# Attention opening: q of batch 0 in 24-token runs, a whole first FFN chunk, and a new order of the instructions

## The chip, the cores and the metric

The kernel runs on one core of a Trainium2 chip. A core has five engines that run their own instruction lists and wait for one another by semaphores: TensorE (PE, with its weight loads shown apart as PEld), VectorE (DVE), ScalarE (ACT), GpSimd (POOL) and SyncE (SP). The metric is the device time of one execution in microseconds, as the median of the runs shown.

## The reference

Two parts are computed, one behind the other. The attention works on 4 batches, 8 heads, 768 tokens and 64 dimensions, with the tokens in 8 blocks of 96. A small matrix per head says how key and value blocks are mixed:

```python
P = sort_net
for _ in range(5):
    P = P - np.max(P, axis=-1, keepdims=True)
    P = np.exp(P)
    P = P / (np.sum(P, axis=-1, keepdims=True) + 1e-09)
    P = P / (np.sum(P, axis=-2, keepdims=True) + 1e-09)
k_sorted = np.einsum('bhij,bhjcd->bhicd', P, k_b)
v_sorted = np.einsum('bhij,bhjcd->bhicd', P, v_b)
scores = scale * np.matmul(q_b, k_sb.transpose(0, 1, 2, 4, 3))
attn = softmax(scores)            # within the block of 96 only
x = attn @ v_sb                   # to (3072 tokens, 512)
```

The feed-forward part takes these 3,072 rows of 512:

```python
h = x @ w_in                      # 512 -> 2048
g = np.maximum(h, 0.0) + alpha * np.minimum(h, 0.0)
out = g @ w_out                   # 2048 -> 512
```

## The kernel before

All work goes by 32 groups, one for each batch and block (group 8 is the first of batch 1). For a group PE makes two kinds of scores. In the near form, used for batch 0, the scores are made twice: once as rows for the maximum (L715 in two halves of the array, DVE takes the maximum at L721) and once turned, with the negative maximum added by a product (L736, L727), so that one exp on ACT (L759) gives the turned matrix that the product with V needs (L768). In the far form, used from batch 1 on, PE makes them once (L712), ACT makes eight exps (L748), and SP turns the result by DMA (L753). DVE divides by the row sums (L776, L779), and xq is turned on PE (L794) or by DMA (L787) into xT.

Ahead of it stand the mixing matrices. The Sinkhorn loop (L518 to L532) alternates between ACT (the exp, L521) and DVE. Its result Pb is spread by eight products (L539) into BDK, with which batch 0's K is mixed and turned in one step: six units of 16 products (L600, written to PSUM) and one copy each (L372, into KT). V of batch 0 goes the same way in eight units (L653 copies, L674 products, L372 copies into VS). For later batches the mixing takes units of 8 products (K: L616, L629, L640; V: L658, L669, L684); a "piece" below is one such unit.

q of batch 0 is loaded by POOL (L397) and turned on PE in six units of 16 products against the identity (also L600), with an ACT copy each (L372, into QTz). q of later batches is loaded by POOL in eight pieces, one for each head (L401, into QN), and turned by six DMA transposes on SP (L409), each of which needs all eight pieces.

The feed-forward part works on chunks of groups. FFN1 (L823) is one unit of four products for each of the 16 slices of the 2,048 columns, on 192 tokens (two groups) or 384 (four groups). ACT takes relu(−h) (L833) and DVE makes the result (L836). FFN2 (L863) sums 16 products of 512 columns for each 128 tokens, in four groups of four, and the result is copied out (L372) and stored by SP (L877).

Loads are issued by POOL (q L397; K and V L419 and L435; w_in in four parts L908; w_out in two parts L913) and go through one queue in order.

The order is written out by hand. SEQ is a list of the numbers of all operations; each engine runs its operations in the order of that list, and a letter behind a number picks the engine where two can do it. The costs and priorities that each operation carries in the code have no part in it. WARM puts filling products ahead of operations of PE: 512-wide products of the identity (L808) into a bank that nobody reads. BURST is a run of small products of zeros (L889) at the very start. PSUM banks are named psS, psH, psO, psYP and so on.

Of the kernel before, what the change touches and what calls it, by code (L numbers as in the profile page):

```python
# [7 lines left out]
AP = bass.AP  # L8
# [19 lines left out]
BURST = 130  # L28
# [8 lines left out]
0 7 11 2 3 1 4 8 9 22 42 28 14 43 44 45 46 19 47 18 5 48 49 50 15 51 39 52 53 6 54 55 25 56 138 57 58 23 29 59 12p  # L37
60 61 130 62 63 64 31 65 32 66 37 13 67 68 89 69 83 81 70 84 71 87 131 10 91 88 85 132 72 40 73 90 74 133 75 86 76
41 77 82 134 78 79 92 26 80 147 93 148 102 94d 103a 104 95 105a 100 98 96a 99a 97d 109d 106p 35 111d 112d 108p 34
16 101a 36 38 33 107p 158 149 114 115d 146 110p 118 250p 159 116 248p 119a 120 113p 121d 124 30 117d 160 135 125a  # L40
249p 254p 24 136 161 122 137 144 150 126 127a 143 123d 145 128 151 129d 253p 247d 20 17 152 162 21 163 164 141 153
177 154 140 155 165 156 142 166d 184 157a 167 185 196 193 168 186 169 194 197 195 199 198 187 202 170 27 203 205
200 204 188 201 214 206 220 215 217 189 218 207 221 219 222 226 216 229 190 227 223 230 273 228 224 171 208 231 225
235 191 236 238 192a 237 232 239 261 251 262 209 313p 233 252a 240 210 263 347p 211 139 255 241 270 234 212 403 264
256a 213d 291 404 301d 271 242 175 259 292 258p 274 260a 257p 272 265 352p 267 243 266 279 244 311p 293 280 268
300p 281 282 269 312p 294 245 174 304d 285 310p 246d 275 286 351p 283 287 284 338 348p 302 339 295 305p 303a 314
288 296 315 306 289 316 340 307a 290 176 297 320 341 317 276 318 178 321 319 298 322 379 299a 308 380 323 179 309a
342 326 324 343 349 344 327 381 350a 325 328 345 353 382 346d 329 354d 332 330 383 333 331 357 277a 334 180 335
# [982 lines left out]
```

## Time and profile before

| | |
|---|---|
| median of 3 runs | 238.37 us (237.72 to 238.66) |
| span of the profiled execution | 236.6 us (the page gives no other time for it) |
| PE busy | 229.2 us, 97% of the span |
| DVE, ACT, POOL busy | 169.8, 151.6, 73.0 us |
| first score product (L715) | 17.72 us |
| first FFN1 product (L823) | 28.71 us |
| first FFN2 product (L863) | 36.40 us |
| first score product of group 8 (L712) | 56.88 us |

Times in the profile are microseconds from the start of the span. A timeline row has the start, the duration, the engine, the line, what is written from what, the shape and the count; in brackets stands how long the engine was idle before it and what released it, where that was long enough to be shown. "issue" as a releaser means that the profile shows nothing that the engine waited for. Matmuls overlap, so a row's duration is longer than its step to the next row.

### The profile page before, as it was taken

What the parts mean: (1) busy time and instruction counts of PE and PEld (TensorE: products, weight loads), DVE (VectorE), ACT (ScalarE), POOL (GpSimd) and SP (SyncE); (2) the same over time, 40 slices, a digit from 0 to 9 for tenths busy, and PEclk for the clock granted to TensorE, in tenths of its full rate; (3) what the DMA queues carried; (4) which work ended last, traced back from release to release, by engine and by line L of the source; (5) the groups of instructions that cost most, each with busy time, mean ns of one, the idle gap of its engine ahead of it and who ended that gap; (6) DMA issues with size and microseconds to landing.
All of it is one profiled execution on the core that took longest, in us unless ns stands there. A gap on an engine that the chain in (4) does not pass through costs nothing.

```text
span 236.6 us, 6266 instructions
## 1 busy us (share of the span) xinstructions
PE 229.2 (97%) x2532; PEld 142.2 (60%) x2532; DVE 169.8 (72%) x354; ACT 151.6 (64%) x423; POOL 73.0 (31%) x139
## 2 busy tenths in 40 slices
PE   7998998999999999999999999999999999999995
PEld 3446676687666666556566665655555555555543
DVE  4748796989899997868887667676766587744350
ACT  4475265587887988886678786756864646453332
POOL 7958812915659620338590020000000000000000
PEclk9999999999999999999999999999999999999999
DMA  5999999999989999899998796542642323400033
GB/s 96 212 213 168 211 217 202 179 209 158 191 88 167 152 120 173 119 210 166 165 111 114 188 164 135 98 90 52 125 92 82 97 50 79 140 0 1 0 133 135
DMA packets 71453, 31.36 MB, mean 133 GB/s; under 512 B 64504, under 2 KB 65280, under 8 KB 71424
## 3 DMA queue, kind: packets, MB, share of 16 engines
q0 software_dynamic: 22896, 13.63, 42.0%
q1 hardware_dynamic: 48528, 17.33, 37.8%
q8 instruction: 20, 0.33, 0.5%
q14 instruction: 9, 0.07, 0.1%
HBM read 27.28 MB, written 6.29 MB: 142 GB/s over the span
## 4 chain that ended last, share of the span: by engine, by line
PE 76%; DMA 17%; POOL 6%; issue 1%; ACT 0%; POOLq 0%
PE psH L823 31%; PE psYP L863 28%; DMA w_out_bf<-in_moe_w_out_dram 10%; PE psS L863 3%; PE psS L712 3%; DMA VST<-in_v_dram 3%; PE psO L768 3%; PE psYP L669 2%; DMA ET<-Esb 2%; PE psYP L629 1%; DMA QTz<-QN 1%; POOL w_in_bf L908 1%; PE psO L863 1%; PE psS L727 1%; POOL VDz L456 1%; PE psO L794 1%
## 5 line engine op out<-in xcount | busy, mean ns | idle before, releaser
L836 DVE SCALAR_TENSOR_TENSOR hT<-t,omaT,psH 128x384 bf16<-128x384 f32 (+1 forms) x139 | 77.4, 571 | 36.6 <-ACT t L833 35.1
L823 PE MATMUL psH<-xT,w_in_bf 128*128 128x384 bf16 (+1 forms) x556 | 96.9, 311 | 0.0
L833 ACT ACTIVATE t<-psH 128x384 f32<-128x384 f32 (+1 forms) x139 | 63.1, 461 | 50.3 <-PE psH L823 49.2
L863 PE MATMUL psYP<-w_out_bf,hT 128*128 128x512 bf16 x336 | 83.2, 379 | 1.3 <-DMA w_out_bf<-in_moe_w_out_dram 1.3
L823 PEld LDWEIGHTS psH<-xT,w_in_bf 128*128 128x128 bf16 x556 | 49.5, 98 | 28.9 <-DVE hT L836 1.6
L863 PEld LDWEIGHTS psYP<-w_out_bf,hT 128*128 128x128 bf16 x336 | 30.8, 98 | 30.1 <-DMA w_out_bf<-in_moe_w_out_dram 1.8
L748 ACT ACTIVATE Esb<-psS,nf 96x96 bf16<-96x96 f32 x192 | 46.1, 345 | 2.0 <-DVE nf L721 2.0
L721 DVE TENSOR_REDUCE nf<-psS 96x8 f32<-96x768 f32 x24 | 22.8, 951 | 6.4 <-PE psS L712 6.0
L658 POOL COPY VDz<-VST 64x192 f32<-64x192 f32 x39 | 20.4, 524 | 20.3 <-DMA VST<-in_v_dram 16.6
L779 DVE TENSOR_TENSOR xq<-psO,rec 96x512 bf16<-96x512 f32 x31 | 21.2, 683 | 0.5
L401 POOL DMA_DIRECT2D QN<-in_q_dram x24 | 19.8, 833 | 3.3 <-DMA QTz<-QN 2.7
L616 POOL COPY KSz<-KS 64x256 f32<-64x256 f32 x28 | 11.1, 397 | 31.6 <-PE psYP L629 19.8
L712 PEld LDWEIGHTS psS<-KT,QTz 128*96 128x96 bf16 x192 | 12.1, 124 | 3.3 <-DMA QTz<-QN 0.2
L768 PEld LDWEIGHTS psO<-VS,ET 112*128 112x128 bf16 x248 | 11.1, 98 | 3.6 <-ACT ET L759 0.2
L808 PE MATMUL psYP<-identb 128*128 128x512 bf16 x40 | 12.8, 453 | 0.4 <-ACT identb L372 0.4
L372 ACT ACTIVATE VS<-psYP 112x512 bf16<-112x512 f32 x15 | 10.3, 687 | 4.2 <-PE psYP L669 2.2
L768 PE MATMUL psO<-VS,ET 112*128 112x65 bf16 x248 | 12.7, 194 | 0.0
L712 PE MATMUL psS<-KT,QTz 128*96 128x96 bf16 x192 | 12.6, 208 | 0.0
L372 ACT ACTIVATE KT<-psYP 128x512 bf16<-128x512 f32 x15 | 9.0, 599 | 2.8 <-PE psYP L629 1.8
L669 PEld LDWEIGHTS psYP<-BDV,VDz 128*128 128x128 bf16 x192 | 8.2, 98 | 2.7 <-POOL VDz L658 0.4
L372 ACT ACTIVATE outstg<-psYP 128x512 f32<-128x512 f32 x13 | 7.7, 604 | 3.2 <-PE psYP L863 3.2
L669 PE MATMUL psYP<-BDV,VDz 128*128 128x64 bf16 x192 | 9.5, 193 | 0.2 <-POOL VDz L658 0.2
(137 smaller groups left out, 198.8 us busy)
## 6 DMA issues: line engine op xcount, KB each, us to landing
out_dram<-outstg SPq DMA_DIRECT2D x23, 256.0 KB, 2.5
KS<-in_k_dram POOLq DMA_DIRECT2D x3, 768.0 KB, 13.3
QN<-in_q_dram POOLq DMA_DIRECT2D x24, 96.0 KB, 4.4
w_in_bf<-in_moe_w_in_dram POOLq DMA_DIRECT2D x4, 512.0 KB, 17.3
w_out_bf<-in_moe_w_out_dram POOLq DMA_DIRECT2D x2, 1024.0 KB, 23.9
VST<-in_v_dram POOLq DMA_DIRECT2D x4, 384.0 KB, 17.6
hT<-in_q_dram POOLq DMA_DIRECT2D x1, 768.0 KB, 7.6
VST<-in_v_dram POOLq DMA_DIRECT2D x1, 768.0 KB, 11.1
```

Of the source, the lines that this page charges most:

```text
L372: return e.activation(o, i, ACTF.Copy) if e is nc.scalar else e.tensor_copy(o, i)
L658: G.add(SHIFT, lambda e, o2=o2, i2=i2: e.tensor_copy(o2, i2), {"dve": 424, "pool": 525}, r=vst, w=[("VDz", u % VSL, th)], prio=prio)
L669: inst = e.matmul(AP(t, off + dd * 64, [[row, 128], [1, 64]]), AP(VDz, (u % VSL * 4 + dd // 2) * 256 + dd % 2, [[VSL * 1024, 128], [2, 128]]),
L712: inst = e.matmul(o, AP(QTz[n], hp * 3072 + h4 * 768 + i * 96, [[6144, 128], [1, 96]]), AP(KT[n], (h4 * 8 + i) * bk, [[ld, 128], [64, 2], ...
L721: G.add(DVE, lambda e: e.tensor_reduce(AP(nx, 0, [[8, 96], [4, 2], [1, 4]]), AP(psX, 0, [[1024, 96], [512, 2], [96, 4], [1, 96]]), AxisLis ...
L748: inst = e.activation(AP(Esb[me], p * 128, [[1024, 96], [64, 2], [1, 48]]), AP(psX, (p // 4) * 512 + (p % 4) * 96, [[1024, 96], [48, 2], [ ...
L768: inst = e.matmul(AP(psZ, hp * 512 + h4 * 68, [[1024, 128], [1, 65]]), AP(ET[me] if far else ET[m], pos(h4, hp) * 96, [[800, nk], [1, 128] ...
L779: G.add(DVE, lambda e: e.tensor_tensor(out=AP(xq[me], 0, [[512, 96], [256, 2], [64, 4], [1, 64]]), in0=AP(psZ, 0, [[1024, 96], [512, 2], [ ...
L823: inst = e.matmul(AP(pt, poff, [[1024, 128], [1, n]]), AP(w_in_bf, kt * DFF + ft // 2 * 256 + ft % 2, [[KT_TILES * DFF, 128], [2, 128]]), ...
L833: G.add(ACT, lambda e: e.activation(AP(t1[tb], 0, [[384, 128], [1, n]]), AP(pt, poff, [[1024, 128], [1, n]]), ACTF.Relu, scale=-1.0), t_ac ...
L836: G.add(DVE, lambda e: e.scalar_tensor_tensor(out=AP(hT, ft * RING + tok % RING, [[FT_TILES * RING, 128], [1, n]]), in0=AP(t1[tb], 0, [[38 ...
L863: inst = e.matmul(AP(bank[0], bank[1], [[1024, 128], [1, n]]), AP(hT, ft * RING + tok % RING, [[FT_TILES * RING, 128], [1, 128]]), AP(w_ou ...
```

## The change

In words:

- BURST falls from 130 to 81 products, and WARM from 43 filling products to 19 (four more, in the attention of group 1, stay).
- q of batch 0 is loaded as two pieces of 1,536 values for each partition instead of one of 3,072, so a partition holds runs of 24 tokens. Six units of 8 products turn it, each 64 columns of q against the whole 128-wide identity, instead of 16 products of 64 by 64.
- The rows of VS get 66 values instead of 65 (one is padding). The copy of V of batch 0 (now L664) may also stand on ACT, where two do. The division may stand on ACT too, though none does.
- The first FFN chunk is four groups instead of two chunks of two. For its first 8 slices the unit is still done in halves of two groups, for the other 8 whole.
- SEQ is another list, on all engines. Numbers of costs and priorities in the code differ too.

The opening on PE, before: the burst (L889), filling (L808), q units (L600 from hT), the spread (L539), K units (L600 from KS), the first scores (L715).

```order
L889 MATMUL psS<-bz 32x32 x130
L808 MATMUL psYP<-identb 128x512 x14
...
L808 MATMUL psYP<-identb 128x512 x8
L539 MATMUL psYP<-Pb,sel 128x8 x8
L808 MATMUL psYP<-identb 128x512 x2
L600 MATMUL psH<-BDK,KS 64x64 x16
L600 MATMUL psYP<-BDK,KS 64x64 x16
L808 MATMUL psYP<-identb 128x512 x2
L600 MATMUL psH<-BDK,KS 64x64 x32
L600 MATMUL psO<-BDK,KS 64x64 x32
L808 MATMUL psYP<-identb 128x512 x6
L715 MATMUL psH<-KT,QTz 96x96 x8
```

The same with the change (the lines are now L909, L828, L540, L601 and L727):

```order
L909 MATMUL psS<-bz 32x32 x81
L828 MATMUL psYP<-identb 128x512 x13
...
L828 MATMUL psYP<-identb 128x512 x4
L540 MATMUL psYP<-Pb,sel 128x8 x8
L601 MATMUL psH<-BDK,KS 64x64 x16
L601 MATMUL psO<-BDK,KS 64x64 x16
...
L601 MATMUL psYP<-BDK,KS 64x64 x16
L601 MATMUL psH<-BDK,KS 64x64 x16
L828 MATMUL psYP<-identb 128x512
L727 MATMUL psH<-KT,QTz 96x96 x8
```

The filling between the units is gone, and the K units follow one another without it.

The part of POOL's order with the loads of batch 1's q (QN, L401), the first V load of batch 2 (L435, the one behind them) and K of batch 2 (L419), before:

```order
L401 DMA QN<-in_q_dram 128x6x64 x3
L616 COPY KSz<-KS 64x8x32
L461 MEMSET QN 128x6x32 x2
L401 DMA QN<-in_q_dram 128x6x64 x3
L658 COPY VDz<-VST 64x48x4 x2
L401 DMA QN<-in_q_dram 128x6x64
L435 DMA VST<-in_v_dram 64x3072
L419 DMA KS<-in_k_dram 128x3072
```

With the change (QN L402, V L436, w_out L933, V copies L670, K L420):

```order
L402 DMA QN<-in_q_dram 128x6x64
L928 DMA w_in_bf<-in_moe_w_in_dram 128x2x1024
L436 DMA VST<-in_v_dram 64x3072
L933 DMA w_out_bf<-in_moe_w_out_dram 128x4x1024
...
L670 COPY VDz<-VST 64x48x4 x4
L462 MEMSET QN 128x6x32
L670 COPY VDz<-VST 64x48x4 x9
L402 DMA QN<-in_q_dram 128x6x64 x2
L670 COPY VDz<-VST 64x48x4
L436 DMA VST<-in_v_dram 64x3072
L670 COPY VDz<-VST 64x48x4 x2
L420 DMA KS<-in_k_dram 128x3072
```

The V load of batch 2 now stands ahead of six of the eight q loads, and the last two q loads stand behind thirteen V copies. Elsewhere on POOL the first w_in load moved ahead of K of batch 1, and the first w_out load ahead of the third and fourth w_in loads.

PE just ahead of the first score product of group 8, before (the FFN1 units are halves, 192 wide):

```order
L823 MATMUL psH<-xT,w_in_bf 128x192 x8
L768 MATMUL psO<-VS,ET 128x65 x8
L669 MATMUL psYP<-BDV,VDz 128x64 x8
L823 MATMUL psH<-xT,w_in_bf 128x192 x8
L863 MATMUL psYP<-w_out_bf,hT 128x512 x4
L712 MATMUL psS<-KT,QTz 96x96 x8
```

With the change (FFN1 L843, FFN2 L883, V pieces L681, scores L724):

```order
L843 MATMUL psYP<-xT,w_in_bf 128x384 x4
L843 MATMUL psH<-xT,w_in_bf 128x384 x8
L883 MATMUL psYP<-w_out_bf,hT 128x512 x4
L681 MATMUL psYP<-BDV,VDz 128x64 x8
L724 MATMUL psS<-KT,QTz 96x96 x8
```

Over the whole stretch from the first instruction to this place, V pieces of batch 1 rise from 3 to 9, xq turns from 7 to 8, and FFN2 groups fall from 5 to 4; the FFN1 units are 16 halves and 11 whole ones, where they were 29 halves.

On ACT the q copies and KT copies moved, before:

```order
L372 ACTIVATE QTz<-psH 128x64x8
L372 ACTIVATE QTz<-psO 128x64x8
L521 ACTIVATE P<-P 32x64
...
L372 ACTIVATE QTz<-psS 128x64x8
L372 ACTIVATE KT<-psYP 128x32x2x8
L372 ACTIVATE KT<-psH 128x32x2x8 x2
L372 ACTIVATE KT<-psO 128x32x2x8 x2
```

and with the change, where L522 is the exp:

```order
L372 ACTIVATE QTz<-psO 128x128x4
L522 ACTIVATE P<-P 32x64
...
L372 ACTIVATE QTz<-psH 128x128x4 x2
L372 ACTIVATE QTz<-psO 128x128x4
L372 ACTIVATE QTz<-psS 128x128x4 x2
L372 ACTIVATE KT<-psO 128x32x2x8 x2
L372 ACTIVATE KT<-psH 128x32x2x8
```

One q copy instead of two stands ahead of the last exp, and three KT copies instead of five stand on ACT; the other three are on DVE.

The diff, cut to its core:

```diff
-BURST = 130
+BURST = 81
 WARM = """
-89:14:y 79:8:y 93:2:y 104:2:y 158:6:y 118:1:y 128:4:y 162:1:y 153:3:h 205:1:y 207:1:y
+87:13:y 79:4:y 158:1:y 160:1:y
 """
 SEQ = """
-0 7 11 2 3 1 4 8 9 22 42 28 14 43 44 45 46 19 47 18 5 48 49 50 15 51 39 52 53 6 54 55 25 56 138 57 58 23 29 59 12p
+0 7 2 12d 3 1 4 10 8 11 9 5 40 39 42 6 43 16 28 44 130 45 46 47 19 48 13 49 50 51 52 53 54 138 55 56 21 57 58
...
-    VS = [sb("VS%d" % n, [112, 64, 65], BF16) for n in range(2)]
+    VS = [sb("VS%d" % n, [112, 64, 66], BF16) for n in range(2)]
...
-            G.add(POOL, lambda e: e.dma_start(AP(hT, 8192, [[HR, 128], [1, 3072]]), AP(q.tensor, 0, [[3072, 128], [1, 3072]])),
+            G.add(POOL, lambda e: e.dma_start(AP(hT, 8192, [[HR, 128], [1536, 2], [1, 1536]]),
+                                                   AP(q.tensor, 0, [[1536, 128], [HB // 2, 2], [1, 1536]])),
...
-        G.add(PE, pairs(hT, 8192, u, identb, 0, 128, bank), 372, r=[("QS", 0), "identb"], w=keys, prio=prio)
-        o = AP(QTz[0], 8 * u, [[6144, 128], [96, 32], [48, 2], [1, 8]])
-        i = AP(t, off, [[row, 128], [2, 32], [1, 2], [64, 8]])
+            for c in range(4):
+                for hp in range(2):
+                    inst = e.matmul(AP(t, hp * 64 * row + off + c * 128, [[row, 64], [1, 128]]),
+                                    AP(hT, 8192 + hp * 1536 + (4 * u + c) * 64, [[HR, 128], [1, 64]]), identb[:, :])
...
+        o = AP(QTz[0], 4 * u, [[6144, 128], [24, 128], [1, 4]])
+        i = AP(t, off, [[row, 128], [1, 128], [128, 4]])
...
+            G.add(("pool", "dve", "act"), lambda e: copy(e, ob, ib) if e is nc.scalar else e.tensor_copy(o, i),
...
-    chunks = [(0, 2), (2, 4)] + [(c, c + 4) for c in range(4, NG, 4)]
+    chunks = [(c, c + 4) for c in range(0, NG, 4)]
+    HALF = 8
...
+            if ga == 0 and ft < HALF:
+                ffn_plan.append((2.5 + ft / 8, 0, (0, 2, ft)))
+                ffn_plan.append((v0 + ft / 8, 0, (2, 4, ft)))
+            else:
+                ffn_plan.append((v0 + w * ft / FT_TILES, 0, (ga, gb, ft)))
```

More of the change, by code (lines that the diff above doesn't have):

```diff
@@ L514, in dv @@
         def dv(fn, r, w):
-            G.add(DVE, fn, 210, r=r, w=w, prio=pr)
+            G.add(DVE, fn, 191 if w[0] in ("rs", "cs") and w == r else 255 if w == ["cs"] else 208, r=r, w=w, prio=pr)
         for it in range(5):
@@ L562, in f @@
             return inst
-        G.add(PE, f, 100 * rows, r=["Pb", "selk"] + [("xT", 1)] * late, w=PSP, prio=prio)
+        G.add(PE, f, 130 * n + 110, r=["Pb", "selk"] + [("xT", 1)] * late, w=PSP, prio=prio)
         for y, mk in ((0, "mkj"), (1, "mkjV"))[:1 + late]:
@@ L678, in prep_v @@
         if b:
-            G.add(PE, f, 250, r=[("VDz", u % VSL, th) for th in range(2)] + [("BDV", b)], w=keys, prio=prio)
+            G.add(PE, f, 232, r=[("VDz", u % VSL, th) for th in range(2)] + [("BDV", b)], w=keys, prio=prio)
         else:
-            G.add(PE, f, 374, r=[("VD", u), "VD0", ("BDK", 0)], w=keys, prio=prio)
-        o = AP(VS[n], 8 * u, [[64 * 65, 112], [65, 64], [1, 8]])
+            G.add(PE, f, 277, r=[("VD", u), "VD0", ("BDK", 0)], w=keys, prio=prio)
+        o = AP(VS[n], 8 * u, [[64 * 66, 112], [66, 64], [1, 8]])
         i = AP(t, off, [[row, 112], [1, 64], [64, 8]])
-        G.add(EITHER, lambda e: copy(e, o, i), {"act": 685, "dve": 690}, r=keys + [("VS1", n)], w=[("VS", n, u)],
+        G.add(EITHER, lambda e: copy(e, o, i), {"act": 610, "dve": 690}, r=keys + [("VS1", n)], w=[("VS", n, u)],
               prio=prio)
@@ L776, in attention, with div @@
         G.add(DVE, lambda e: e.reciprocal(AP(rec[m], 0, [[8, 96], [4, 2], [1, 4]]),
-                                          AP(psZ, 64, [[1024, 96], [512, 2], [68, 4]])), 200,
+                                          AP(psZ, 64, [[1024, 96], [512, 2], [68, 4]])), 197,
               r=banks_o, w=[("rec", m)], prio=prio)
-        G.add(DVE, lambda e: e.tensor_tensor(
-            out=AP(xq[me], 0, [[512, 96], [256, 2], [64, 4], [1, 64]]),
-            in0=AP(psZ, 0, [[1024, 96], [512, 2], [68, 4], [1, 64]]),
-            in1=AP(rec[m], 0, [[8, 96], [4, 2], [1, 4], [0, 64]]), op=AluOpType.mult), t_dve(512),
-            r=banks_o + [("rec", m)], w=[("xq", me)], prio=prio)
+        def div(e):
+            if e is not nc.scalar:
+                return e.tensor_tensor(
+                    out=AP(xq[me], 0, [[512, 96], [256, 2], [64, 4], [1, 64]]),
+                    in0=AP(psZ, 0, [[1024, 96], [512, 2], [68, 4], [1, 64]]),
+                    in1=AP(rec[m], 0, [[8, 96], [4, 2], [1, 4], [0, 64]]), op=AluOpType.mult)
+            inst = None
+            for p in range(8):
+                inst = e.activation(AP(xq[me], p * 64, [[512, 96], [1, 64]]),
+                                    AP(psZ, p // 4 * 512 + p % 4 * 68, [[1024, 96], [1, 64]]), ACTF.Copy,
+                                    scale=rec[m][:, p:p + 1])
+            return inst
+        G.add(EITHER if g < 12 else DVE, div, {"act": 1350, "dve": 686}, r=banks_o + [("rec", m)], w=[("xq", me)], prio=prio)
         o2 = AP(xT, g * BLK % XR, [[KT_TILES * XR, 128], [XR, 4], [1, 96]])
@@ L827, in f @@
             return inst
-        op = G.add(PE, f, t_pe(*[(n, 128)] * 4), r=[("xT", g % 16) for g in range(ga, gb)] + [("w_in", ft // 8 * 2 + x) for x in range(2)],
+        op = G.add(PE, f, {192: 330, 384: 650}[n], r=[("xT", g % 16) for g in range(ga, gb)] + [("w_in", ft // 8 * 2 + x) for x in range(2)],
               w=keys, prio=prio)
@@ L890, in burst @@
         return inst
[L891 removed]
+    G.add(PE, burst, 1240, r=["bz"], w=["psSw", "psS0", "psS1"], prio=-120)
     load_q(0, -98)
```

218 lines of the change are left out of this document (111 added, 107 removed).

## The prediction

> **What bounds the kernel now.** I read the first part of the page, then the busy time by stretches, then the waits of TensorE, and last its timeline in the first 60 us.
>
> ```profile
> span 236.6 us, 6266 instructions
> PE 229.2 (97%) x2532; PEld 142.2 (60%) x2532; DVE 169.8 (72%) x354; ACT 151.6 (64%) x423; POOL 73.0 (31%) x139
> ...
> 0.00:10.00 10.00, 7.93 (x212) 4.05 (x213) 5.92 (x32) 3.57 (x9) 8.43 (x20) 1.00 0.75 143
> 10.00:20.00 10.00, 9.39 (x244) 5.74 (x237) 5.90 (x21) 6.86 (x16) 7.34 (x13) 1.00 1.03 204
> ...
> 30.00:40.00 10.00, 8.70 (x129) 6.93 (x128) 7.49 (x21) 5.62 (x16) 0.52 (x1) 1.00 1.17 208
> ...
> 60.00:80.00 20.00, 20.00 (x229) 12.86 (x228) 18.83 (x36) 16.70 (x53) 15.03 (x27) 1.00 1.22 147
> ```
>
> The columns after the stretch are PE, PEld, DVE, ACT, POOL, granted clock, DMA share and GB/s. From 60 us PE is never free: what is left to do there, at PE's pace, sets the end. Before 60 us PE looks busy too, but part of that is filling (the 512-wide identity products of L808), and the longest wait is a load's:
>
> ```profile
> PE psYP L863 <- DMA w_out_bf<-in_moe_w_out_dram: 1.3, 1, 1.3
> ```
>
> The place that I take as the hinge is the first score product of batch 1 (L712, group 8). It needs batch 1's q, which POOL loads in eight pieces (L401) and SP turns by DMA (L409).
>
> ```profile
> 50.95 11.79 SPq L409 DMA_TRANSPOSE QTz<-QN  x5
> ...
>   PEld psS L712: 0.2, 1
> ...
> DMA to landing us min/median/max: 4.7/6.0/7.0
> ...
> 56.02 1.03 PE L863 MATMUL psYP<-w_out_bf,hT 128*128 128x512 bf16 x4
> 56.88 0.52 PE L712 MATMUL psS<-KT,QTz 128*96 128x96 bf16 x8
> 57.24 0.34 PE L794 MATMUL psO<-identb,xq 96*128 96x96 bf16 x4
> 57.41 0.82 PE L823 MATMUL psH<-xT,w_in_bf 128*128 128x192 bf16 x8
> 58.07 1.03 PE L863 MATMUL psYP<-w_out_bf,hT 128*128 128x512 bf16 x4
> 58.94 0.40 PE L669 MATMUL psYP<-BDV,VDz 128*128 128x64 bf16 x8
> 59.17 0.49 PE L823 MATMUL psH<-xT,w_in_bf 128*128 128x192 bf16 x4
> ```
>
> SP waits for the last of the eight loads until 50.95, the first turn lands some 5.8 us later, and the weight load of L712 waits 0.2 for it: load, turn and PE arrive together. The starts also give PE's paces: 0.87 for a group of four 512-wide products (58.07 to 58.94), 0.33 for four 192-wide (57.41 to 58.07 is two), 0.23 for a V or K piece, 0.17 for a turn of xq.
>
> **The change, part by part.** First the hinge, since it decides.
>
> *Work ahead of the hinge.* Counted in the two orders, the changed list puts ahead of the first score product of group 8: nine V pieces of batch 1 instead of three (+6 × 0.23 = 1.38), eight xq turns instead of seven (+0.17), four FFN2 groups instead of five (−0.87), and of FFN1 16 half units and 11 whole ones instead of 29 halves. For a whole unit of 384 columns I use
>
> ```profile
> 183.06 1.30 PE psH L823 x8
> 184.36 1.73 PE psYP L863 x8
> ```
>
> so 0.65 each: 16 × 0.33 + 11 × 0.65 − 29 × 0.33 = +2.86. Together +3.54. The first chunk as a whole becomes 8 × 2 × 0.33 + 8 × 0.65 = 10.48 instead of 32 × 0.33 = 10.56 (−0.08). All else on PE behind the hinge is the same work, so what is left there falls by **3.6 us**.
>
> *When the hinge can start: q.* In the changed POOL order the second w_in and w_out loads, the K and V loads and q of batch 1 are the same in sum ahead of the last q load, except that one V load of batch 2 (64 rows, half a tensor) now goes out before them. Its price comes from the loads of w_in, which pass through a full queue:
>
> ```profile
> 10.08 2.13 POOL L908 DMA_DIRECT2D w_in_bf<-in_moe_w_in_dram  x3
> ...
> w_in_bf<-in_moe_w_in_dram POOLq DMA_DIRECT2D x1, 512.0 KB, 16.3
> ...
> w_in_bf<-in_moe_w_in_dram POOLq DMA_DIRECT2D x1, 512.0 KB, 19.9
> ...
> 12.19 24.17 DMA w_out_bf<-in_moe_w_out_dram
> ```
>
> Three are issued 0.71 apart from 10.08; the first lands at 26.4, the third at 31.4, so 512 KB take 2.5 us and the V load's 384 KB 1.9. The last q load lands at 50.95 + 1.9 = 52.8. The turn then takes between 4.7 and 6.0 us; I take 5.0, below the 5.8 of today, because the K load of batch 2 that shares the queues with it today is now issued later: 57.8, range 57.5 to 58.8. Against 56.88 that is **+0.9**.
>
> *When PE gets there.* This decides only if it is later than 57.8. Rows of the opening:
>
> ```profile
> 8.93 0.44 PE L600 MATMUL psS<-identb,hT 64*64 64x64 bf16 x16 [0.52 <-DMA hT<-in_q_dram]
> 9.66 0.60 ACT L372 ACTIVATE QTz<-psH 128x512 bf16<-128x512 f32 x1 [1.15 <-PE psH L600]
> 10.17 0.60 ACT L372 ACTIVATE QTz<-psO 128x512 bf16<-128x512 f32 x1
> 10.66 0.24 ACT L521 ACTIVATE P<-P 32x64 f32<-32x64 f32 x1
> ...
> 10.57 1.90 PE L808 MATMUL psYP<-identb 128*128 128x512 bf16 x8
> 13.27 0.44 PE L600 MATMUL psH<-BDK,KS 64*64 64x64 bf16 x16
> 16.11 0.28 PE L600 MATMUL psO<-BDK,KS 64*64 64x64 bf16 x6 [0.51 <-issue]
> 13.75 0.69 DVE L372 CAST KT<-psH 128x512 bf16<-128x512 f32 x1 [0.62 <-PE psH L600]
> 16.43 1.08 ACT L372 ACTIVATE KT<-psO 128x512 bf16<-128x512 f32 x2 [0.36 <-PE psO L600]
> 17.72 0.38 PE L715 MATMUL psH<-KT,QTz 64*96 64x96 bf16 x8
> 22.33 0.71 PE L674 MATMUL psO<-BDK,hT 128*64 128x64 bf16 x32 [0.52 <-issue]
> 28.71 0.83 PE L823 MATMUL psH<-xT,w_in_bf 128*128 128x192 bf16 x8
> 36.40 1.04 PE L863 MATMUL psYP<-w_out_bf,hT 128*128 128x512 bf16 x4 [1.27 <-DMA w_out_bf<-in_moe_w_out_dram]
> ```
>
> The last Sinkhorn exp (10.66) stands behind two q copies on ACT; in the changed list behind one, 0.4 to 0.5 earlier, so the K products start near 12.84. Then today five of six KT copies queue on ACT (0.54 each, to 17.51). Three on ACT and three on DVE (0.69 today) end near 15.2, and the first scores start near 15.2 instead of 17.72. From there to the first FFN1 product the changed list does 0.8 more scores work (group 2's second scores) and eight fewer filling products (five for thirteen, 8 × 0.216 = 1.7, with 0.216 from 1.73 for eight 512-wide). PE alone would be at FFN1 by 25.3, but it needs the second w_in load. That stays sixth in the queue, so 26.4, and the exp, division and copy between scores and FFN1 don't shrink: I take 26.7.
>
> The two "issue" waits need a guess. They stand exactly 128 products apart, 6.2 us apart in time, and the page has this row:
>
> ```profile
> q8 instruction: 20, 0.33, 0.5%
> ```
>
> 20 packets of 16 KB for 5,064 loads and products of PE is one per 256, or 128 products: a block of PE's code that arrives late while the loads fill the queues. The changed opening moves the boundaries to the start of the q products, the fifth K unit and the fourth V unit. If each block comes some 6 us behind the boundary before it, there are again two waits, of 0 to 1.2 each. FFN1 then starts between 26.7 and 28.7. The Trainium skill, "Runtime: NRT & Kernel Launch", section "Instruction fetch mechanics", says that crossing such a 16 KiB block costs one bump of a DMA tail, "mostly hidden". Here the 0.51 and 0.52 disagree with "hidden". By that rule FFN1 would start at 26.7, by the rows up to 28.7.
>
> From FFN1 to the hinge: w_out's first load moves ahead of two w_in loads, lands at 36.4 − 2 × 2.5 = 31.4 and is wanted near 34, so the 1.27 goes. The work between grows by 3.54 − 0.8 − 0.43 (two filling products) = 2.3. Arrival: 56.88 − 2.0 − 1.3 + 2.3 = **55.9**, at worst 57.9. So q is the later one, and PE waits 0 to 2 us there, about 1.4.
>
> *What costs nothing.* 49 fewer burst products and one fewer filling product end before q lands, where PE idles 0.52. The q products: 8 of 128 columns for 16 of 64. If two halves of the array run side by side, a unit keeps its 0.25; if not, 8 × 0.216 / 4 = 0.43, six units +1.1 at most, and they are then done by 11.5, while PE waits for the Sinkhorn result until near 12; without that cover it would be 1.1 on the K stage. Pieces of 3 KB instead of 6 KB in q's load: no row has the like. Its bytes take 3.7 us at the pace of w_in; a quarter more would be +0.9, and the other end is −0.5, the idle before q today. Both fall on a front that has 1.9 to spare before q of batch 1; I take 0. conv_v on ACT and the 66-wide rows of VS lie beside PE work.
>
> *Sum*: 236.6 + 0.9 − 3.6 = 233.9. The page gives no clock time of its own; the median lies 1.8 above the span. **235.6 us.** The bounds of the turn give 235.3 to 236.6.
>
> **Rivals.**
>
> *q is early and the front decides.* If the last q load isn't late (it goes out where another queue has room) or the turn is short, the hinge starts at PE's own arrival, 55.9 to 57.5: 232.0 to 233.6 span, about 234.2 us. For: the row of DMA share has empty stretches after 52 us today. Against: the loads are in one queue, in order.
>
> *The gain is given back behind 58 us.* DVE is busy 18.83 of 20 us in the stretch from 60, ACT 16.70. With FFN1 further ahead, DVE's work per PE work there could become the bound, or the V loads of batch 3 come too late for an earlier PE:
>
> ```profile
> 94.52 1.56 POOL VST L435 x3
> 96.08 7.59 DMA VST<-in_v_dram
> ```
>
> Stretch 100 to 120 has PE busy 19.75 of 20, so this wait is 0.25 today. If PE comes 2.7 earlier and the load doesn't, 1 to 2 us return: 237. Against: the load's release hangs on work that comes earlier too.
>
> *q is later still.* The last two q loads now stand on POOL behind thirteen V copies that need free slots, that is V products of PE. If they are issued after 50, the queue runs dry before them and the hinge moves past 60: 60.5 gives 238.3, no change. Against: by the pace of the queue the copies' data lands near 35, and the loads ahead keep the queue full until 48.
>
> *Slower: PE falls back to half its clock.* Filling products at 2.80 take 5.62 for 14, later 1.90 for 8:
>
> ```profile
> 2.80 5.62 PE L808 MATMUL psYP<-identb 128*128 128x512 bf16 x14 [0.37 <-ACT identb L372]
> ```
>
> so PE doubles its pace during the opening. With 24 filling products fewer, PE idles near 11.5, 12.4, 14.8 and 16.2, each 0.5 to 0.8 us. If those send it back, some 10 us of useful products before FFN1 take 20, less the 4 us of waits that this swallows: FFN1 near 32.7, the hinge at 61.9 and the end at 236.6 + 5.0 − 3.6 = 238.0, so 239.8 us; it decides from an FFN1 later than 28.6. Against: PE already idled 0.5 at 8.4 and 15.9 with the pace kept. The Trainium skill, "TensorE: Matmul & The Clock Gate", Part 1, lets the clock fall only after an idle window of about 3.4 us; by that rule, with no such gap, this rival has no chance at all, and no stretch of this trace holds one that long.
>
> **How the numbers follow.** Forecast 0.62 (235.3 to 236.6); q early 0.09 (234.2); given back later 0.12 (237); q later still 0.10 (238.3); half clock 0.07 (239.8). A measurement here can tell about 0.5%, 1.2 us: faster is under 237.2, slower over 239.6. Faster: 0.62 + 0.09 + 0.08 + 0.01 = 0.80; same: 0.04 of the third and 0.09 of the fourth, 0.13; slower 0.07. The range goes from 233.8, below the q-early case, to 237.9, which leaves out the half clock and most of the fourth.
>
> **What would show it.** In the changed profile: the first score product of group 8 starts at 57.5 to 58.8 with 0.5 to 2 us of idle put down to the q turn, and SP's first q turn starts near 52.8; no wait for w_out; first scores near 15.2; first FFN1 between 26.7 and 28.7; two short "issue" waits at the fifth K unit and in the V run. PE's idle from 60 on stays near today's. The forecast is wrong if PE arrives later than q, if the hinge is past 59.5, or if PE's idle behind it grows by over 1 us.

## The result, and the profile after

The changed kernel takes 235.05 us (median of 4 runs, 234.56 to 235.79), the kernel before, run beside it, 238.05 us (4 runs). The ratio is 0.9875, with a 95% interval of 0.9849 to 0.9901: faster by 1.25%. A second set of four runs on another occasion gave 234.96 us and 0.9852 (0.9811 to 0.9893). The forecast was 235.6 us, within 233.8 to 237.9.

The page of the profiled execution after, its first lines and the one of PE's code packets:

```profile
span 233.6 us, 5916 instructions
...
PE 222.7 (95%) x2350; PEld 137.5 (59%) x2379; DVE 171.7 (74%) x360; ACT 148.1 (63%) x414; POOL 67.2 (29%) x126
...
q8 instruction: 19, 0.31, 0.5%
```

PE issues 2,379 weight loads instead of 2,532 (the count of products lacks a few records). The waits of PE in the same execution, the longest behind q's load (the w_out row and the two "issue" rows are gone, and no row names the q turn):

```profile
PE psYP L540 <- DVE Pb L533: 0.8, 1, 0.8
...
PE psH L748 <- DVE nm L733: 0.5, 1, 0.5
PE psH L727 <- DVE KT L372: 0.5, 1, 0.5
```

PE's timeline at the places of the prediction:

```profile
13.15 0.44 PE L601 MATMUL psH<-BDK,KS 64*64 64x64 bf16 x16 [0.38 <-DVE BDK L544]
15.68 0.38 PE L727 MATMUL psH<-KT,QTz 64*96 64x96 bf16 x8 [0.50 <-DVE KT L372]
27.65 0.49 PE L843 MATMUL psH<-xT,w_in_bf 128*128 128x192 bf16 x4
35.45 0.81 PE L883 MATMUL psYP<-w_out_bf,hT 128*128 128x512 bf16 x3
57.25 0.40 PE L681 MATMUL psYP<-BDV,VDz 128*128 128x64 bf16 x8
57.48 0.54 PE L724 MATMUL psS<-KT,QTz 128*96 128x96 bf16 x8
```

SP's timeline with the first q turn:

```profile
51.34 7.14 SPq L410 DMA_TRANSPOSE QTz<-QN  x4
```

The view of the DMAs for the microsecond of its issue, with the median time to landing at the end:

```profile
QTz<-QN SPq DMA_TRANSPOSE x1, 5.5
```

The first score product of group 8, which the prediction calls the hinge, starts at 57.48 instead of 56.88, directly behind the V piece at 57.25. The turn had landed at 51.34 + 5.5 = 56.8. So nothing waits there, and PE itself came last. The V piece at 57.25 is not one of batch 1, as the count before the prediction has it: batch 1 has eight pieces, and this ninth one is the first of batch 2. It needs both V loads of that batch, so the one that was moved ahead of q is wanted there.

One more view, by stretches, shows what no part of the sum had:

```profile
18.00:20.00 2.00, 2.00 (x58) 1.84 (x58) 1.25 (x2) 1.30 (x2) 1.94 (x5) 0.51 1.04 204
20.00:22.00 2.00, 2.00 (x56) 1.82 (x56) 1.93 (x5) 1.00 (x2) 0.78 (x2) 0.63 0.99 199
```

The granted clock (the third number from the end) is 0.51 and 0.63 in these four microseconds, so PE is busy all the time and does little more than half the work. Read in steps of 0.1 us, the clock is at half from 18.05 to 21.46.

### The profile page after: what moved, and what is told of

Read it like the earlier page. It is cut to its first block, busy times and chain, and to the rows that moved or that the text cites. A ratio compares the mean times of both kernels' runs of the same rounds, so it can differ in the third digit from the quotient of the medians.

```text
span 233.6 us, 5916 instructions
## 1 busy us (share of the span) xinstructions
PE 222.7 (95%) x2350; PEld 137.5 (59%) x2379; DVE 171.7 (74%) x360; ACT 148.1 (63%) x414; POOL 67.2 (29%) x126
## 4 chain that ended last, share of the span: by engine, by line
PE 86%; DVE 6%; ACT 4%; issue 2%; POOL 0%; POOLq 0%
PE psH L843 34%; PE psYP L883 30%; PE psS L724 4%; PE psS L883 3%; PE psO L780 3%; PE psYP L681 3%; PE psS L739 2%; PE psYP L638 2%; DVE nm L733 1%; PE psS L748 1%; PE psO L883 1%; PE psO L686 1%; PE psYP L843 1%; PE psO L814 1%; DVE KT L372 1%
## 5 line engine op out<-in xcount | busy, mean ns | idle before, releaser
L856 DVE SCALAR_TENSOR_TENSOR hT<-t,omaT,psH 128x384 bf16<-128x384 f32 (+1 forms) x131 | 75.2, 587 | 39.7 <-ACT t L853 38.3
L843 PE MATMUL psH<-xT,w_in_bf 128*128 128x384 bf16 (+1 forms) x524 | 95.9, 317 | 0.0
L853 ACT ACTIVATE t<-psH 128x384 f32<-128x384 f32 (+1 forms) x131 | 61.6, 478 | 48.7 <-PE psH L843 46.3
L883 PE MATMUL psYP<-w_out_bf,hT 128*128 128x512 bf16 x308 | 79.0, 379 | 1.5
L843 PEld LDWEIGHTS psH<-xT,w_in_bf 128*128 128x128 bf16 x524 | 47.1, 98 | 30.2 <-DVE hT L856 4.4
L883 PEld LDWEIGHTS psYP<-w_out_bf,hT 128*128 128x128 bf16 x336 | 30.9, 98 | 28.8 <-ACT outstg L372 0.3
L670 POOL COPY VDz<-VST 64x192 f32<-64x192 f32 x29 | 15.3, 527 | 23.9 <-PE psYP L681 15.5
L402 POOL DMA_DIRECT2D QN<-in_q_dram x24 | 19.8, 835 | 3.1 <-DMA QTz<-QN 2.8
L372 ACT ACTIVATE VS<-psYP 112x512 bf16<-112x512 f32 x18 | 10.8, 602 | 5.2 <-PE psYP L681 3.8
L724 PEld LDWEIGHTS psS<-KT,QTz 128*96 128x96 bf16 x192 | 11.5, 124 | 3.8 <-ACT Esb L760 1.4
L724 PE MATMUL psS<-KT,QTz 128*96 128x96 bf16 x192 | 12.7, 209 | 0.0
L681 PE MATMUL psYP<-BDV,VDz 128*128 128x64 bf16 x192 | 9.6, 193 | 0.0
L681 PEld LDWEIGHTS psYP<-BDV,VDz 128*128 128x128 bf16 x192 | 7.9, 98 | 2.8 <-ACT VS L372 0.7
L771 ACT ACTIVATE ET<-psS 112x768 bf16<-112x768 f32 x7 | 5.7, 809 | 5.2 <-PE psS L739 5.2
L883 PE MATMUL psS<-w_out_bf,hT 128*128 128x512 bf16 (+1 forms) x47 | 8.7, 325 | 0.1
```

The lines of the kernel that those rows point to most:

```text
L372: return e.activation(o, i, ACTF.Copy) if e is nc.scalar else e.tensor_copy(o, i)
L402: G.add(POOL, lambda e, h=h: e.dma_start(AP(QN, h * 128 + (h // 4) * 64, [[6144, 128], [1024, 6], [1, 64]]), AP(q.tensor, b * HB + h * S * ...
L681: inst = e.matmul(AP(t, off + dd * 64, [[row, 128], [1, 64]]), AP(VDz, (u % VSL * 4 + dd // 2) * 256 + dd % 2, [[VSL * 1024, 128], [2, 128]]),
L724: inst = e.matmul(o, AP(QTz[n], hp * 3072 + h4 * 768 + i * 96, [[6144, 128], [1, 96]]), AP(KT[n], (h4 * 8 + i) * bk, [[ld, 128], [64, 2], ...
L843: inst = e.matmul(AP(pt, poff, [[1024, 128], [1, n]]), AP(w_in_bf, kt * DFF + ft // 2 * 256 + ft % 2, [[KT_TILES * DFF, 128], [2, 128]]), ...
L853: G.add(ACT, lambda e: e.activation(AP(t1[tb], 0, [[384, 128], [1, n]]), AP(pt, poff, [[1024, 128], [1, n]]), ACTF.Relu, scale=-1.0), 170 ...
```

## Experiments

All of them have one yardstick, three numbers of the profiled execution: the start of the first FFN1 product (front), the start of group 8's first score product (hinge), and the span. Times are medians; ratios are to the kernel before, run beside them.

| kernel | front | hinge | span | hinge to end | median | ratio (95%) |
|---|---|---|---|---|---|---|
| before | 28.71 | 56.88 | 236.6 | 179.7 | 238.05 | |
| changed | 27.65 | 57.48 | 233.6 | 176.1 | 235.05 | 0.9875 (0.9849 to 0.9901) |
| changed, again (a0_same) | 26.95 | 56.77 | 232.8 | 176.0 | 234.96 | 0.9852 (0.9811 to 0.9893) |
| e1_fill | 28.07 | 57.90 | 234.1 | 176.2 | 235.80 | 0.9902 (0.9879 to 0.9924) |
| e2_q_first | 28.67 | 59.25 | 235.4 | 176.2 | 235.60 | 0.9898 (0.9865 to 0.9932) |
| e3_fill_q_first | 28.18 | 59.34 | 235.5 | 176.2 | 236.62 | 0.9932 (0.9904 to 0.9959) |
| e4_q_late | 27.71 | 57.61 | 236.6 | 179.0 | 235.58 | 0.9893 (0.9865 to 0.9920) |
| a1_old_q | 33.61 | 64.49 | 240.5 | 176.0 | 241.23 | 1.0123 (1.0051 to 1.0195) |
| a2_burst130 | 31.72 | 61.54 | 239.8 | 178.3 | 240.53 | 1.0080 (1.0053 to 1.0108) |
| a3_burst33 | 28.95 | 58.77 | 234.8 | 176.0 | 236.51 | 0.9910 (0.9876 to 0.9945) |
| a4_fill_earlier | 27.30 | 58.02 | 234.1 | 176.1 | 236.05 | 0.9906 (0.9876 to 0.9937) |
| b3_burst81 | 31.70 | 58.42 | 238.8 | 180.4 | 240.75 | 1.0102 (1.0068 to 1.0136) |
| b4_new_q | 32.35 | 58.99 | 239.3 | 180.3 | 240.66 | 1.0081 (1.0054 to 1.0108) |
| b2_less_fill | 31.59 | 58.45 | 237.9 | 179.5 | 241.78 | 1.0126 (1.0070 to 1.0182) |

Executions of e2, e3, a1, a2, a3 and b2 scatter by 1.7 to 4 us, so one profile there shows a mechanism and not the median. The profiled execution of e4 took 238.49, its other four 235.5: it lost 2.5 us at 105 us, and is read up to the hinge only. a0 to a3 ran beside one another. The e runs and a4 had no run of the changed kernel beside them, and the intervals of e1, e2, e4 and a4 overlap with those of the changed kernel, so differences of 0.5 to 1 us from it are weak evidence there.

### Is q's turn what the hinge waits for?

e2_q_first moves one load in POOL's order, e4_q_late another:

```diff
 e2: ... q of heads 1, 0, 5, 3 ... V copies ... q of heads 7, 6
-349 (V load of batch 2, first half) ahead of the second w_out load
+349 behind the last q load
 e4:
+348 (V load of batch 2, other half) ahead of the q loads of heads 7 and 6
```

> The changed kernel with the V load of batch 2 put back behind the last q load of batch 1 on POOL. Theory of the hinge: the last q load lands 1.5 earlier, near 49.9, and the first turn near 55.4; PE arrives at 57.5 as before where its clock falls in the opening, so the span stays at 233.6, and it falls to 232.5 to 233 in executions where the clock doesn't fall. Rival (the q turn is what the hinge waits for): the hinge moves 1 to 1.5 earlier, span near 232.3 in all executions. Rival (the V load is wanted early): a wait for V of batch 2 appears and the span grows.

> The changed kernel with one more V load of batch 2 put ahead of the last two q loads of batch 1. Theory of the hinge: the last q load lands 1.9 later, near 53.2, the first turn near 58.5, PE waits about 1.0 for it at the first score product of group 8, and the span grows by that 1.0 to 234.6. Rival (q's lateness is hidden or given back by less waiting later): span stays at 233.6.

In e2 the last q load didn't come earlier. POOL's timeline in the changed kernel, then in e2:

```profile
46.94 0.51 POOL L670 COPY VDz<-VST 64x192 f32<-64x192 f32 x1 [1.13 <-PE psYP L681]
47.31 1.71 POOL L402 DMA_DIRECT2D QN<-in_q_dram  x2
...
48.01 0.51 POOL L668 COPY VDz<-VST 64x192 f32<-64x192 f32 x1 [1.13 <-PE psYP L679]
48.38 1.71 POOL L400 DMA_DIRECT2D QN<-in_q_dram  x2
```

The view of the DMAs issued there in e2:

```profile
QN<-in_q_dram POOLq DMA_DIRECT2D x2, 96.0 KB, 3.2
```

The last two q loads are issued behind a V copy that waits for PE (L679, in the changed kernel L681, is the V piece that frees its slot), and land 3.2 us later. In the changed kernel the time to landing is the same 3.2, issue at 47.3 and 48.2, landing at 51.3. So POOL's place behind the thirteen V copies sets q's time, not the bytes ahead of it, and a load taken out of the queue buys nothing. (A load put directly ahead of them, as in e4, does count: 5.8 us to landing.)

It even costs something, and the rival that the V load is wanted early is borne out in this profile. PE's timeline, SP's timeline and the view of the DMAs:

```profile
58.90 0.41 PE L679 MATMUL psYP<-BDV,VDz 128*128 128x64 bf16 x8 [0.42 <-DVE VDz L668]
59.25 0.56 PE L722 MATMUL psS<-KT,QTz 128*96 128x96 bf16 x8
...
52.69 8.09 SPq L408 DMA_TRANSPOSE QTz<-QN  x4
...
QTz<-QN SPq DMA_TRANSPOSE x1, 6.5
```

PE waits 0.42 for a copy on DVE, which itself waited 0.80 for the V load of batch 2. With the V loads now beside it the turn took 6.5 us and landed at 59.2, just ahead of the hinge at 59.25. Both came last there, 0.75 later than PE alone would have been (its front at 28.67 plus the 29.83 of the next part).

In e4 SP's timeline has the turn at 54.29, 3 us later than in the changed kernel:

```profile
54.29 5.47 SPq L408 DMA_TRANSPOSE QTz<-QN  x4
```

The hinge still started at 57.61, for the view of the DMAs says:

```profile
QTz<-QN SPq DMA_TRANSPOSE x1, 3.3
```

With no bulk load beside it the turn took 3.3 us instead of 5.5. It landed at 57.6, directly ahead of the hinge, so the lateness used up all the slack that q has in the changed kernel (0.6 in its first profile, 0.3 in the second) and cost less than 0.1 us. Both expectations failed in their numbers: q has some slack, and a lateness of the load is partly made up by the turn. e4's four other executions stand at 235.5, half a microsecond above the changed kernel; a stop of PE at 20.83 (further down) could account for that as well as q.

### What sets PE's arrival

> The changed kernel itself, once more, so that the four variants before it and the three with it stand on the same footing. Two readings are open. If PE's clock falls in the opening as in the first profile, the first FFN1 product starts near 27.7 with no wait for code; if it doesn't, a wait of 0.8 to 0.9 for code stands two products into the fourth V unit and a second one at the spread of batches 1 to 3, and FFN1 starts near 27.2 to 27.7 as well. Either way the first score product of group 8 comes at 57 to 57.6 and the span is 233 to 233.7, the time 235.0 to 235.5.

Here the clock stayed at 1.00, and neither stop for code was more than a stretched row:

```profile
19.75 0.96 PE L686 MATMUL psO<-BDK,hT 128*64 128x64 bf16 x32
...
25.91 0.67 PE L748 MATMUL psS<-QTz,KT 64*112 64x96 bf16 x8
26.95 0.49 PE L843 MATMUL psH<-xT,w_in_bf 128*128 128x192 bf16 x4
56.77 0.54 PE L724 MATMUL psS<-KT,QTz 128*96 128x96 bf16 x8
```

Each of the first two rows is some 0.25 longer than its like (0.71 for 32, 0.41 for 8). From front to hinge there are 29.82 us here, and 29.83, 29.83, 29.82 and 29.82 in the first profile, e1, a2 and a3. In the others more lies between: in e2 the two waits above, in e4 q's turn (29.90), and in a1, a4 and e3 (30.7 to 31.2) a clock that is still at half behind the front (in e3 q's turn as well, which lands at 59.3). So in the changed kernel the hinge is the front plus a constant where neither happens, and the end is the hinge plus 176.1. The two profiles of the one kernel show it best: the front is 0.70 later in the first, the hinge 0.71, the end 0.8.

### The code blocks

The change takes 121 PE products out of the opening in three lots: 49 of the burst, 48 of q, 24 of filling. Each lot was put back or taken out alone:

```diff
 a2 (changed kernel):  BURST = 81  ->  130
 a3 (changed kernel):  BURST = 81  ->  33
 a1 (changed kernel):  q of batch 0 loaded and turned in the old form (96 products of 64x64)
 b3 (kernel before):   BURST = 130 ->  81
 b4 (kernel before):   q of batch 0 loaded and turned in the new form (48 products of 64x128)
 b2 (kernel before):   WARM = "89:14:y 79:4:y 158:1:y"
```

> The changed kernel with q of batch 0 in its old form: one run of 48 tokens for each partition, 96 products of 64 by 64 instead of 48 wider ones. All else as changed. Theory of the code blocks (PE's code comes in blocks of 128 products, each some 6.2 us behind the boundary before it while the loads fill the queues): 48 more products put the boundaries at the second K unit, the second V unit and the transposed alpha, with waits near 1.5 and 2.5 us there instead of 0.8 and 0.8; the first FFN1 product slips to 29.5 to 31, the first score product of group 8 to 59 to 60, and the span grows by 2, to 235.5. Rival (the wider products only save PE time ahead of the Sinkhorn result, where PE waits anyway): no change, span 233.6. Rival (the old form's six units are faster on PE, so it gains): span below 233.3.

> The changed kernel with 130 burst products as before, 49 more. They end before the first filling product, so they cost PE no time of their own. Theory of the code blocks: the boundaries move as in the run with the old q, so the same two waits and the same loss of about 2 us, span near 235.5. Rival (the burst lies in idle time): no change, 233.6.

> The changed kernel with 33 burst products, 48 fewer. Theory of the code blocks: the boundaries move 48 products later in the work, to the group scores behind the first K units (17.1) and the last V run; the block behind that comes near 23.3, a single wait of some 2 us at the last V run, and FFN1 starts near 28.5, so fewer products lose too: span 234 to 234.6. Rival (fewer instructions always come sooner): FFN1 near 26.5 and span near 233. Rival (the clock needs the burst): half clock past 8 us, q late, and a loss of over 1 us that shows in the clock.

> The kernel before with 81 burst products instead of 130, nothing else. Theory of the code blocks: the two stops move from the last K unit and the seventh V unit to the fifth product of the second V unit and the fifteenth of the last one, 49 products later in the work each, with waits near 0.7 and 1.7 us instead of 0.5 and 0.5; FFN1 starts near 30 instead of 28.7. Behind it PE waits 1.27 for w_out today, which swallows that: the first score product of group 8 stays near 57 and the span at 236.6 to 237. So the shorter burst alone gains nothing; it gains only where the rest of the opening is cut to fit. Rival (fewer instructions are better by themselves): FFN1 near 28 or earlier. Rival (the longer stop lets the clock fall): half clock behind it, span 238 or more.

> The kernel before with the new form of q of batch 0 (24-token runs, 48 wider products), nothing else. Theory of the code blocks: 48 products fewer ahead of the K units, so nearly the same stops as with the shorter burst (the fourth product of the second V unit, the fourteenth of the last), FFN1 near 30, span 236.6 to 237. Rival (the wider products gain by themselves): FFN1 earlier than 28.5 and a span of 236 or less.

> The kernel before with 24 filling products fewer (14 before q, 4 before the spread, 1 before the first scores, and the 4 of group 1 stay). Theory of the code blocks: the stops move to the first scores, without a wait there, and to the fourth V unit, with one of about 2 us; FFN1 starts near 28.7 and w_out's wait swallows what differs: span 236.3 to 237. Rival (each filling product costs its 0.2 us): 24 x 0.216 = 5 us less. Rival (the filling holds the clock): granted clock of about 0.5 for some us between 15 and 25, FFN1 past 30, span 237 to 239.

In a1, a2, b3 and b4 every stop came at or within two products of where the count put it; in b2 it came in the sixth V unit of PE's order, where the fourth was named, and the stop of some 2 us that was expected in a3 didn't come. PE's timeline of a1:

```profile
19.27 0.20 PE L677 MATMUL psYP<-BDK,hT 128*64 128x64 bf16 x2
20.95 0.59 PE L677 MATMUL psYP<-BDK,hT 128*64 128x64 bf16 x14 [1.49 <-issue]
...
27.10 0.28 PE L931 MATMUL psYP<-identf,alphaR 8*128 8x8 f32 x1 [1.05 <-issue]
```

of a2:

```profile
18.27 0.20 PE L686 MATMUL psYP<-BDK,hT 128*64 128x64 bf16 x1
19.08 0.42 PE L686 MATMUL psYP<-BDK,hT 128*64 128x64 bf16 x15 [0.61 <-issue]
...
25.71 0.40 PE L940 MATMUL psYP<-identf,alphaR 8*128 8x8 f32 x2 [1.95 <-issue]
```

of b3:

```profile
20.61 0.39 PE L674 MATMUL psYP<-BDK,hT 128*64 128x64 bf16 x12 [1.25 <-issue]
...
27.12 0.25 PE L674 MATMUL psO<-BDK,hT 128*64 128x64 bf16 x4 [0.48 <-issue]
```

of b4:

```profile
19.56 0.39 PE L683 MATMUL psYP<-BDK,hT 128*64 128x64 bf16 x12 [0.89 <-issue]
...
26.27 0.26 PE L683 MATMUL psO<-BDK,hT 128*64 128x64 bf16 x5 [1.75 <-issue]
```

and of b2:

```profile
23.82 0.48 PE L674 MATMUL psO<-BDK,hT 128*64 128x64 bf16 x18 [1.44 <-issue]
```

A run of 16 is cut after the second product (a1) or the first (a2), where nothing in the program changes, and the two stops of a kernel lie 6.1 to 6.7 us apart, as they do before (16.11 and 22.33). Products that do nothing, issued in the first 2 us, move the stops. Two more things in the traces show that this is PE's code and not the data. Counted in the weight loads, a stop stands behind number 350 or 351, or behind number 477, in all ten kernels that have one (before, a1, a2, b2 to b4, e1 to e4), whatever the work there is. And all seventeen stops end 2.2 to 2.6 us after a packet of the instruction queue (q8) has started: in a2, for example, packets start at 16.6 and 23.3 and PE goes on at 19.08 and 25.71.

The size of a stop isn't fixed by PE's list alone. e2 and e4 have the list of the changed kernel on PE, and stop for 0.78 and 0.87 at the place where a0_same has 0.25: their packet starts at 18.2 and 18.3, that of a0_same at 17.7.

The loss was larger than the stops. a1 lost 6.3 us against the changed kernel run beside it (a0_same) where I had expected 2, a2 5.6; b3, b4 and b2, expected to lose nothing, lost 2.4, 2.4 and 3.5 against the kernel before. a3 lost 1.6 where 0.4 to 1.0 was expected, by the clock and with no stop at all. So none of the three lots gains by itself: tried alone in the kernel before they cost 0.8 to 1.3%. Only with the new order are they part of a gain. 121 products are nearly one block of 128, so the boundaries behind the opening return to nearly the same work. Whether that number or the new order makes them harmless isn't told apart by these runs.

In the kernel before, the wait for w_out stood as a buffer between front and hinge. b3's front is 3.0 later and its hinge 1.5, b4's 3.6 and 2.1. In the changed kernel that load is early, and the whole of a late front goes through.

### The clock

In a1, a2 and a3 the extra loss goes with PE's clock. The stretches of a2:

```profile
16.00:18.00 2.00, 1.46 (x30) 1.00 (x24) 1.90 (x5) 0.95 (x2) 1.33 (x3) 1.00 1.07 182
18.00:20.00 2.00, 1.39 (x54) 1.21 (x54) 0.54 (x2) 1.31 (x2) 1.94 (x4) 0.86 1.07 214
20.00:22.00 2.00, 2.00 (x44) 1.82 (x44) 1.77 (x5) 0.62 (x1) 0.80 (x2) 0.50 0.98 196
...
24.00:26.00 2.00, 0.28 (x2) 0.29 (x2) 0.09 (x2) 0.41 (x1) 1.82 (x5) 0.50 1.11 207
26.00:28.00 2.00, 1.73 (x19) 1.18 (x20) 1.10 (x4) 0.00 (x0) 1.83 (x5) 0.50 1.12 213
```

and of a3, which has no stop but the longest idle time ahead of the spread:

```profile
10.00:12.00 2.00, 0.57 (x3) 0.08 (x1) 1.83 (x12) 1.25 (x4) 1.63 (x5) 1.00 1.10 224
...
14.00:16.00 2.00, 1.85 (x59) 1.28 (x55) 1.53 (x4) 1.58 (x3) 0.40 (x1) 0.58 1.01 194
16.00:18.00 2.00, 1.81 (x26) 1.12 (x24) 1.57 (x3) 0.95 (x2) 1.58 (x3) 0.50 1.08 175
```

Behind some microseconds in which PE is busy for 60 to 75% of the time (a2), or for 30% of two microseconds (a3), the clock is half for 10.2 us in both. In a1 it is half from 9.4 to 12.8, behind a wait of 2.13 for q's load and before any stop, and again from 19.6 to 36.7. In steps of 0.1 us every fall in the ten profiles that have one lasts 3.4 us or a multiple: 3.4 in the changed kernel, e2, e3, a4, b3 and b4, 3.4 and 6.8 in b2, 10.2 in a2 and a3, 3.4 and 17.1 in a1. One step of 3.4 us at half takes 0.7% off the mean clock of an execution, so 0.993, 0.979 and 0.957 are one, three and six steps.

The clock isn't the whole of the extra loss. Two executions of b3 at a clock of 1.00 took 240.3 and 241.0, one of b4 240.0, and the kernel before beside them 238.3 at 0.993. They left no trace, so where they lost it stays open.

Three kernels put filling where PE idles. In e1 and e3 there are eight more filling products, in a4 three are moved:

```diff
 e1, e3: -87:13:y 79:4:y 158:1:y 160:1:y
         +87:13:y 79:7:y 93:1:y 158:3:y 160:3:y        (e3 has e2's edit too)
 a4:     +87:13:y 79:5:y 158:1:y 160:3:y   and   warm(e, 4, (psH, 0))  ->  warm(e, 1, (psH, 0))
```

> The changed kernel with eight more filling products where its PE idles in the opening (three before the spread, one before the K units, two more before the first scores, two more behind them). In the changed kernel PE's granted clock was 0.51 and 0.63 in the stretches 18 to 20 and 20 to 22 us. Theory of the hinge (the end is the start of group 8's first score product plus the work left, and that product starts at the later of PE's arrival and the landing of the q turn, 56.9): the clock stays at 1.00, the first FFN1 product starts near 26.5 instead of 27.65, but the hinge moves only from 57.5 to 56.9: span 233.0, about 0.6 less. Rival (what the front gains, the end gains): 1.2 less, span 232.4. Rival (the clock's fall has nothing to do with idle PE time): the clock falls again, span 233.6 or a little more.

> Both of the edits before: eight more filling products and the V load behind q. Theory of the hinge: neither the clock nor the turn holds PE up, the hinge starts at PE's arrival, near 56.3, and the span is 232.4, about 1.2 less than the changed kernel's 233.6. If only one of the two mattered, this equals the better of the two alone.

> The changed kernel with three of its filling products moved from group 1's place (near 24 us) to the idle stretches at 11.4 (one) and 16.4 (two); the count of instructions stays. If idle PE time near 10 to 17 is what lets the clock fall in some executions, it falls in none of these, FFN1 starts near 27.0 in all, and the time is 234.6 to 234.9, up to 0.3 less than the changed kernel. If the clock's fall comes from elsewhere, the time is 235.0 and single executions still show a clock of 0.99.

e1 kept the clock at 1.00 and still took 0.7 us more than the changed kernel. Its eight products moved the stops, and both are larger than in a0_same (the first is as large as those of e2 and e4, which have no product more):

```profile
20.30 0.46 PE L739 MATMUL psS<-identb,nm 96*112 96x96 bf16 x6 [0.80 <-issue]
26.96 0.18 PE L558 MATMUL psYP<-Pb,selk 32*128 32x64 bf16 x1 [0.77 <-issue]
```

e3 had stops of 1.16 and 0.52, then a clock of 0.55 at 28 to 30, and its ten executions fall into two groups, near 235.7 and 237.5. The clock doesn't part them: two of the slower five show 1.00. a4 took 1 us more: the idle time that it left near 23 us was followed by the same fall, later:

```profile
22.00:24.00 2.00, 1.18 (x19) 0.81 (x19) 1.31 (x5) 0.60 (x1) 0.83 (x3) 1.00 1.13 216
...
26.00:28.00 2.00, 2.00 (x21) 1.86 (x22) 1.93 (x6) 0.46 (x1) 1.83 (x4) 0.50 1.12 213
```

Idle PE time stands ahead of every fall (in a3, a4 and b2 clearly; in a2 and b3 it comes together with the stops). But it doesn't decide by its amount. From 12 to 18 us PE is busy for 61, 75 and 73% in the changed kernel's first profile, in a0_same and in e4 alike, and the clock fell in the first alone; e4 idled more than either from 8 to 10 and from 20 to 22. In steps of 3.4 us counted back from the fall at 18.05, PE is busy for 64% in the step from 11.2, which no fall follows, and for 70% in the step from 14.6, which one does. What else decides stays open. No variant beat the changed kernel.

## Why the prediction was right, and where not

**The sum held, by its larger term.** The work left behind the hinge was to fall by 3.6 us. The hinge-to-end column falls from 179.7 to 176.1, and it is 176.0 to 176.2 in seven more profiles of the changed kernel's variants (a2 and e4 add waits behind the hinge). With the hinge 0.6 later instead of 0.9 the span is 233.6 where 233.9 was forecast, and 1.7 lie between span and time. Nothing but counted products at quoted paces went into that term.

**The step "when the hinge can start: q" failed.** It said that q comes last, at 57.8, 1.9 later by the bytes of one V load. The last q load landed at 51.3 and not 52.8, the turn at 56.8. What sets it is POOL's order: the loads are issued at 47.3 behind V copies that wait for PE. That rule was in the text as a rival ("q is later still"), with the wrong sign. By the prediction's own sign, "wrong if PE arrives later than q", its mechanism at the hinge failed though its time held.

**The front decided, which was the rival given 0.09.** It promised 55.9 to 57.5 for the hinge and 232.0 to 233.6 for the span; both profiles lie in it (56.77 and 232.8, 57.48 and 233.6, the second at its edge, with the clock at half for 3.4 us). Its chance was too low, because PE's arrival was put at 55.9 when it was 56.8 to 57.5. The terms: front 26.7, measured 26.95 and 27.65; front to hinge 29.2, measured 29.83, since small waits in between (0.36 and 0.24 for a maximum and a KT copy at 30 and 33 us) were counted as no more than today's. So "a front that has 1.9 to spare" was false: it has nothing to spare. That the time came within 0.7 us of the forecast is in part luck: the turn landed 1.0 to 1.4 earlier than forecast, PE arrived 0.9 to 1.6 later, and the two errors nearly cancel at a hinge forecast for 57.8 and measured at 56.8 and 57.5.

**What costs nothing.** That the burst and the q products lie beside other work is right for their own time, and wrong as a price: put back into the changed kernel, 49 burst products cost 5.6 us, 48 q products 6.3. The K stage came nearly as said: K products at 13.15 (12.84), first scores at 15.68 (15.2). Of the two places named for a stop, the fifth K unit shows none, and the V run only the stretched row. The w_out wait is gone as forecast.

**The two rules that were weighed.** By the Trainium skill, "Runtime: NRT & Kernel Launch", section "Instruction fetch mechanics", a block boundary is mostly hidden. The changed kernel's two profiles agree (0.25 each, or nothing); e1 (0.80 and 0.77), a1 (1.49 and 1.05), a2 (0.61 and 1.95), e2 (0.78) and e4 (0.87) don't. By the Trainium skill, "TensorE: Matmul & The Clock Gate", Part 1, the clock falls after an idle window of about 3.4 us, and by that rule, as the prediction says, the rival of the half clock had no chance; it was given 0.07. In the changed kernel's first profile it fell to 0.51 with no idle stretch over 0.85 us between q and there. The rival's mechanism is real; in the changed kernel it costs about 0.8 us of span in some executions (233.6 and 234.1 at a clock of 0.99, 232.8 to 233.5 in the six at 1.00), and a1, a2 and b2, whose executions all show it, are slower than the kernel before.

## What to carry to other kernels

Find the place behind which an engine never waits again, and count what work is left there in the old and the new order: that term can be trusted, and the waits ahead of it matter only as far as they move that place. In an opening where loads fill the queues, count PE's instructions too, not only their time: a product that lies in idle time still moves the boundaries of the code blocks, and the time lost there can be several times the stop itself. Parts of such a change can't be judged one by one; each of the three tried alone was about 1% slower, and together they are part of a gain.

## What was not expected of the hardware

Two stops for PE's code lie 6.1 to 6.7 us and some 128 products apart while the loads run (seven kernels), single stops reach 1.95 us, and each ends 2.2 to 2.6 us after a packet of the instruction queue starts. PE's granted clock can halve without a long gap: in the changed kernel's first profile it did so behind 6 us with busy shares of 61 to 75% and gaps of 0.38 to 0.85 us, while the same shares and much the same gaps left it at 1.00 in a0_same and e4. It then stays at half for 3.4 us or a multiple, up to 17.1 in a1. An SP transpose of q takes 3.3 us from issue to landing with no bulk load beside it (e4), 5.0 and 5.5 with 0.23 and 0.33 MB of loads moved meanwhile (a0_same, changed), and 5.8 to 7.4 with 0.64 to 0.69 MB (before, e2, b4).
